# Where the high and low parts of chunk 3's split operands are issued in the opening of a fused FNet and GEGLU kernel

## The chip, the cores and the metric

The kernel runs on one core of one Trainium2 chip. The metric is the device time of one execution in microseconds (us); a shorter time is better. The engines are named as in the profile: PE is the matrix engine (TensorE), PEld its weight loads, DVE is VectorE, ACT is ScalarE, POOL is GpSimd and SP is SyncE, whose queue issues most of the transfers.

## What is computed

The input x has 2048 rows of 448 columns. Each row is normalized; the normalized rows go through a two-sided Fourier transform of which the real part is kept, and through a gated network, whose output gates the transform.

```
xn = layernorm(x)
a, b = xn @ hid_re.T, xn @ hid_im.T
s = seq_re @ a - seq_im @ b
g = silu((gelu(xn @ w_gate) * (xn @ w_up)) @ w_down)
out = x + s * g
```

w_gate and w_up are 448 by 1792, w_down is 1792 by 448, and all of it is in float32.

## The kernel before

Every float32 operand of a product is kept as two parts: a high part in a reduced format (written by ACT, line 142 in `split`) and a low part that is the remainder (written by DVE, line 143 in `split`). A product is three matmuls: high by high, high by low, and low by high.

The rows of x are four chunks of 512 (c = 0 to 3), and the inner dimension of the network is 14 blocks of 128 (f), taken in pairs. The program has an opening, a middle and an end. The opening turns each chunk (transposes on PE, line 187; copies on ACT; the low part on DVE) and computes the first pair of blocks, f = 0 and 1, for every chunk in the plain way: `gateup(f, c, ...)` makes two sums of 11 matmuls each (line 361), the gate and the up product, each into a PSUM bank, and `act` follows with a gelu of the gate on ACT (line 386), the gated product gelu times up on DVE (line 389), its high part on ACT (line 390) and its low part on DVE (line 391). `act` returns the last three as functions: m, h and l below, with 0 or 1 behind them for f. `down(0, c, ...)` multiplies the result with w_down in four steps kk = 0 to 3 of six matmuls each (line 415), each into one of two banks that take turns, and ACT evicts each bank (line 422) into `po_out`, which is then stored to `gs`. A list of functions, `between`, is called one entry behind each eviction, and so sets what ACT and DVE do between two evictions.

In the middle, from the pair f = 2 and 3 on, two chunks at a time are multiplied by Strassen's scheme (`strassen`, lines 438 and 445). Its operands are combinations of the turned chunks: `combine` makes them on DVE for chunks 0 and 1, and on POOL for chunks 2 and 3 (lines 217 to 224). `t_places` and `v_places` return functions t_split(i) and v_split(i) that split one combination i = 0 to 3 each; the parts go to tiles that the profile calls xt and t_lo (high and low of t) and t_v (both of v). The first unit of Strassen forms x1 to x4 in that order; x2 needs number 1 of t and v, x3 needs 2, x4 needs 0, and 3 comes later. Splitting number 3 of v ends with two small transfers (line 255), since its lower half is copied. The end transforms along the hidden dimension (line 928) and along the sequence (lines 1112 to 1129).

The order on each engine is the order in which the code is written. The mm banks go round in turn over four: gateup(0, 3) has two of them, gateup(1, 3) the other two, then x1 and x2 take the first two again, and x3 and x4 the second two. So x3 needs the gelu of gateup(1, 3) to have read its bank, and x4 its gated product.

The place of the change is the loop over c = 2 and 3 in `fnet_geglu`. At c = 2 it ends with v_split(1) and v_split(2). At c = 3 it computes gateup(0, 3), then down(0, 2) with m0, h0, l0 of chunk 3 and the four t_split between its steps, then gateup(1, 3) with v_split(0) and v_split(3), and then m1. Behind the loop `spill(1)` stores half of chunk 3, and the last down of the pair, down(0, 3), is spread over the first units of Strassen.

Of the kernel before, what the change touches and what calls it, by code (L numbers as in the profile page):

```python
# [45 lines left out]
def fnet_geglu(ctx: ExitStack, tc: tile.TileContext, x, ca, ct, cp, et, wgu, wd, out):  # L46
# [137 lines left out]
    def turn_mm(c, k):  # L184
        pt = tp_tile(f"pt{c}_{k}").rearrange("p (b d) -> p b d", b=4)
        for b in range(4):
            nc.tensor.transpose(pt[:, b], xr[c][:, k, b * P : (b + 1) * P], ident)
        return c, k, pt
# [7 lines left out]
    def turn_split(c, k, pt):  # L196
        sl = slice(k * P, (k + 1) * P)
        h, l = [cols_of(xs(c, lo), c, sl) for lo in range(2)]
        nc.scalar.activation(h, turned(pt, c), AF.Copy)
        for i, v in enumerate(xf[c]):  # L200
            nc.scalar.activation(v[:, :, sl], pt[:, 3 * i :] if i else pt[:, : v.shape[1]], AF.Copy)
        nc.vector.tensor_sub(l, turned(pt, c), h)
# [24 lines left out]
    def t_places(p):  # L227
        if not t_lo:
            t_lo.append(sb.tile([P, 4096], FR, name="t_lo", tag="y"))
        h = [a_x[2 * p + 1][:, o : o + 512] for o in (0, 512, 2048, 2560)]  # L230
        l = [t_lo[0][:, 2048 * p + 512 * i :][:, :512] for i in range(4)]
        t_hl[p][0] = list(zip(h, l))

        def one(i):
            side, k = SPOT[i]
            split(h[i], l[i], xfk(2 * p + side, k))

        return one

    def v_places(p):  # L240
        v = sb.tile([P, 4096], FR, name=f"t_v{p}", tag=f"v{p}")
        vt[p] = v
        hl = []
        for side, k in SPOT:
            hl.append([v[:, 2048 * side + 512 * (k + 2 * a) :][:, :512] for a in range(2)])
        t_hl[p][1] = hl

        def one(i):
            side, k = SPOT[i]
            h, l = hl[i]  # L250
            n = 64 if i == 3 else P
            split(h[:n], l[:n], xfk(2 * p + side, k + 2)[:n])
            if i == 3:
                for a in (h, l):
                    nc.sync.dma_start(a[64:].bitcast(F32), a[:64].bitcast(F32))

        return one
# [7 lines left out]
    def load_s(f, i):  # L265
        raw = a_r[i]
        nc.sync.dma_start(raw[:, :1280], wgu[f].rearrange("p b f -> p (b f)"))
        return raw
# [45 lines left out]
    def prep_s(i, raw):  # L314

        w = slot(i)
        hw = w[:, :1792]
        steps = []

        def part_(a, b):  # L320
            nc.scalar.activation(hw[:, a:b], raw[:, P + a : P + b], AF.Copy)  # L321
            lo = max(a, 384)
            nc.vector.tensor_sub(  # L323
                w[:, 1408 + lo : 1408 + b], raw[:, P + lo : P + b], hw[:, lo:b].bitcast(F32)
            )
            if a == 0:
                nc.vector.tensor_sub(
                    hw[64:, :384], raw[64:, P : P + 384], hw[64:, :384].bitcast(F32)
                )

        names = "x4 x2 x3 s1 a11 a12 a22 b11 r1 s3 s2 s4 r3 r2".split()
        parts = {}
        for n, name in enumerate(names):
            parts[name] = [w[:, n * P : (n + 1) * P]]
            if n > 2:
                parts[name].append(w[:, 1408 + n * P : 1408 + (n + 1) * P])
        return parts, [lambda: part_(0, 896), lambda: part_(896, 1792)]

    def load_d(grp, at):
        rv = at[:, : 2 * D].rearrange("p (f d) -> p f d", f=2)  # L340
        nc.sync.dma_start(
            rv, wd[grp[0] * P : (grp[0] + 2) * P, :].rearrange("(f p) d -> p f d", p=P)
        )
        return rv
# [37 lines left out]
    def act(f, c, pg):  # L382
        acts[0] += 1
        gt = tmp(2 + acts[0] % 2)
        hs = new_hs(f, c)
        nc.scalar.activation(gt, pg[0], AF.Gelu_apprx_tanh)

        return (
            lambda: nc.vector.tensor_mul(gt, gt, pg[1]),
            lambda: nc.scalar.activation(hs[:, 0], gt, AF.Copy),  # L390
            lambda: nc.vector.tensor_sub(hs[:, 1], gt, hs[:, 0]),
        )

    def gateup(f, c, w, between=()):
        pg = gu_ps(f, c)
        for g in range(2):
            gu_mm(pg[g], w, g, c, slice(0, 512))
            if g < len(between):
                between[g]()
        return act(f, c, pg)  # L400
# [28 lines left out]
    def down(gi, c, wdn, between=()):  # L429
        for kk in range(4):  # L430
            down_one(gi, c, wdn, kk)
            if kk < len(between):
                between[kk]()
# [82 lines left out]
    with tc.manual_schedule():  # L516
# [113 lines left out]
        m0, h0, l0 = act(0, 0, pgs[0])  # L630
# [17 lines left out]
        m0, h0, l0 = act(0, 1, pg)  # L648
# [11 lines left out]
        def spill(p):  # L660
            nc.sync.dma_start(xp[p], x_half(p))
# [34 lines left out]
        for c in (2, 3):  # L696
            if c == 2:
                draw = load_d(GROUPS[1], a_st[:, 2304:])
            else:
                s_raw2 = load_s(GROUPS[1][1], 1)  # L700
            m0, h0, l0 = gateup(0, c, ws[0])
            if c == 2:
                turn = lambda k: turn_split(*turn_mm(3, k))
                between = [
                    lambda: (m0(), h0(), norm(2)),
                    lambda: (l0(), norm(3), turn(0), comb.pop(0)()),
                    lambda: (turn(1), comb.pop(0)()),
                    lambda: (turn(2), comb.pop(0)()),
                ]
                between1 = [lambda: (turn(3), comb.pop(0)())]  # L710
            else:
                t_split = t_places(0)
                between = [
                    lambda: (m0(), h0(), t_split(1)),
                    lambda: (l0(), t_split(2)),
                    lambda: t_split(0),
                    lambda: t_split(3),
                ]
                between1 = [lambda: v_split(0), lambda: v_split(3)]
            down(0, c - 1, wdn, between)  # L720
            if c == 2:
                nws[0], steps = prep_s(0, s_raw)
                for f in steps:
                    f()
            m1, h1, l1 = gateup(1, c, ws[1], between1)
            m1()
            if c == 2:
                h1()
                l1()
                comb.pop(0)()  # L730
                v_split = v_places(0)
                v_split(1)
                v_split(2)
        spill(1)
        late = (h1, l1)

# [568 lines left out]
```

## Time and profile before

| what | value |
|---|---|
| median of 3 runs | 783.08 us (782.25 to 785.52) |
| the profiled execution's own time | 782.91 us |
| span of the profiled execution | 781.1 us |
| PE busy | 766.0 us, 98% of the span, 4044 instructions |
| DVE busy | 545.3 us, 70% |
| ACT busy | 363.8 us, 47% |
| POOL busy | 189.1 us, 24% |
| moved by DMA | 170.05 MB, 218 GB/s on average |

The time of an execution is 1.81 us longer than its span. A busy time counts from the start of an instruction to its modelled end; matmuls overlap, so the distance from one start to the next says more about PE's rate than a matmul's own duration. In the rows of the timeline the columns are start, duration, engine, line, operation, what is written and read, the shapes and the count; in brackets stands how long the engine was idle ahead of it and what ended that.

### The profile page before, as it was taken

How to read it: one execution, taken by the hardware profiler on the slowest of the kernel's cores; microseconds unless marked ns; L12 is line 12 of the kernel's file. 1: busy time of each engine (PE TensorE's matmuls, PEld its weight loads, DVE VectorE, ACT ScalarE, POOL GpSimd, SP SyncE). 2: the span in 40 equal slices, each digit the busy share in tenths (PEclk: the TensorE clock that was granted, in tenths of full speed). 3: DMA queues.
4: the chain of work that ended last, by engine and by line, in shares of the span. 5: the costliest groups of instructions: out<-in, count | busy, mean ns of one | idle time of the engine just before them, and what ended most of it. 6: DMA issues, size and time to landing. Idle time of an engine off the chain costs nothing.

```text
span 781.1 us, 11376 instructions
## 1 busy us (share of the span) xinstructions
PE 766.0 (98%) x4044; PEld 686.4 (88%) x4044; DVE 545.3 (70%) x937; ACT 363.8 (47%) x538; POOL 189.1 (24%) x308
## 2 busy tenths in 40 slices
PE   8998999999999999999999999999999999999997
PEld 7887888888888888888889999999999989998896
DVE  7888677545565556456452767988879696969687
ACT  3884545444434435344444585544344433434341
POOL 1119025240421511601011001223222231313130
PEclk9999999999999999999999999999999999999999
DMA  7232656995978968774989972869696959787784
GB/s 289 92 118 88 202 199 131 274 178 108 252 136 219 276 115 218 179 166 81 259 214 247 372 318 82 273 225 329 199 362 192 353 184 315 229 286 226 274 266 180
DMA packets 61371, 170.05 MB, mean 218 GB/s; under 512 B 7425, under 2 KB 40065, under 8 KB 60417
## 3 DMA queue, kind: packets, MB, share of 16 engines
q1 hardware_dynamic: 47440, 108.17, 39.2%
q0 software_dynamic: 13728, 61.02, 34.1%
q8 instruction: 32, 0.52, 0.3%
q14 instruction: 27, 0.21, 0.1%
q10 hardware_dynamic: 144, 0.11, 0.0%
HBM read 127.21 MB, written 70.91 MB: 254 GB/s over the span
## 4 chain that ended last, share of the span: by engine, by line
PE 69%; DVE 15%; DMA 10%; issue 3%; ACT 1%; SPq 0%; DVEq 0%; ACTq 0%
PE x L438 23%; PE po L415 16%; PE ab L928 9%; PE p L1112 8%; PE x L445 4%; PE p L1115 4%; DVE xt L143 4%; DVE e L143 3%; DMA w<-td 3%; PE gu L361 3%; DMA raw<-ct 2%; DMA tmp<-ct 2%; DMA raw<-wgu 1%; DMA raw_d<-ct 1%; DVE cc L1150 1%
## 5 line engine op out<-in xcount | busy, mean ns | idle before, releaser
L438 PE MATMUL x<-xt,w 128*128 128x512 f32 x480 | 149.5, 392 | 0.0
L438 PEld LDWEIGHTS x<-xt,w 128*128 128x128 f32 x480 | 90.1, 188 | 16.1 <-DVE tmp L477 0.4
L422 ACT ACTIVATE po_out<-po 128x448 f32<-128x448 f32 x112 | 60.2, 538 | 83.7 <-PE po L415 82.8
L415 PE MATMUL po<-wd0h,hs 128*128 128x448 f32 x256 | 82.0, 367 | 3.1 <-ACT po_out L422 3.1
L427 POOL DMA_DIRECT2D gs<-po_out x24 | 21.4, 893 | 219.2 <-ACT po_out L422 219.1
L928 PE MATMUL ab<-e,xt 128*128 128x448 f32 x288 | 68.8, 365 | 0.0
L415 PE MATMUL po<-wd,hs 128*128 128x448 f32 x288 | 66.0, 365 | 0.0
L438 PE MATMUL x<-t_v,w 128*128 128x512 f32 x216 | 60.7, 389 | 0.0
L415 PEld LDWEIGHTS po<-wd,hs 128*128 128x128 f32 x288 | 54.1, 188 | 6.7
L928 PEld LDWEIGHTS ab<-e,xt 128*128 128x128 f32 x288 | 54.1, 188 | 4.3
L415 PEld LDWEIGHTS po<-wd0h,hs 128*128 128x128 f32 x256 | 48.1, 188 | 8.4 <-ACT po_out L422 3.5
L1007 POOL DMA_DIRECT2D raw<-sums x45 | 24.8, 552 | 98.4 <-DVE xt L143 29.4
L438 PEld LDWEIGHTS x<-t_v,w 128*128 128x128 f32 x216 | 40.5, 188 | 8.7
L415 PE MATMUL po<-wd0l,hs 128*128 128x448 f32 x128 | 46.9, 366 | 0.0
L142 ACT ACTIVATE e<-raw 128x896 fp32r<-128x896 f32 (+1 forms) x30 | 27.7, 923 | 34.0 <-DVE raw L1014 22.9
L1112 PE MATMUL p<-t_v,wd0l 128*128 128x448 f32 x112 | 37.5, 380 | 3.6 <-DVE cc L1209 3.6
L493 ACT ACTIVATE hs<-tmp 128x512 fp32r<-128x512 f32 x24 | 15.2, 635 | 54.9 <-DVE tmp L491 54.9
L438 PE MATMUL x<-t_lo,w 128*128 128x512 f32 x96 | 37.3, 389 | 0.0
L1007 POOL DMA_DIRECT2D tmp<-sums x39 | 21.5, 552 | 63.6 <-DVE xt L143 27.7
L1112 PE MATMUL p<-w,e 128*128 128x448 f32 x112 | 36.6, 375 | 0.1
L323 DVE TENSOR_TENSOR w<-raw,w 128x512 fp32r<-128x512 f32 (+1 forms) x24 | 21.3, 889 | 19.9 <-ACT w L321 19.9
L143 DVE TENSOR_TENSOR e<-raw,e 128x896 fp32r<-128x896 f32 (+1 forms) x30 | 31.4, 1047 | 4.3 <-ACT e L142 4.0
(317 smaller groups left out, 2014.5 us busy)
## 6 DMA issues: line engine op xcount, KB each, us to landing
gs<-po_out POOLq DMA_DIRECT2D x24, 896.0 KB, 7.9
sums<-ca SPq DMA_DIRECT2D x16, 896.0 KB, 10.7
sums<-ca POOLq DMA_DIRECT2D x16, 896.0 KB, 14.5
t_v<-td SPq DMA_DIRECT2D x24, 448.0 KB, 5.5
w<-td SPq DMA_DIRECT2D x24, 448.0 KB, 7.0
raw<-ct SPq DMA_DIRECT2D x45, 192.0 KB, 4.5
raw<-wgu SPq DMA_DIRECT2D x12, 640.0 KB, 5.5
tmp<-ct SPq DMA_DIRECT2D x39, 192.0 KB, 4.7
```

The source lines that it names most:

```text
L142: nc.scalar.activation(h, src, AF.Copy)
L143: nc.vector.tensor_sub(l, src, h)
L361: nc.tensor.matmul(ps[:, cols], a, xt[:, cols], start=n == 0, stop=n == len(mm) - 1)
L415: nc.tensor.matmul(po[:, :D], hs[:, a, kk * P : (kk + 1) * P], wdn[b][:, i], start=n == 0, stop=n == 5,)
L422: nc.scalar.activation(out_[0][:, kk], po[:, :D], AF.Copy)
L427: nc.gpsimd.dma_start(gv[:, 4 * c : 4 * c + 4], out_[0], accum_op=ALU.add)
L438: nc.tensor.matmul(ps, a[i], b[j], start=first and n == 0, stop=n == 2, skip_group_check=True)
L445: nc.tensor.matmul(ps, a[0], xt, start=False, stop=True, skip_group_check=True)
L928: nc.tensor.matmul(p[:, :D], a, b, start=n == 0, stop=n == len(mm) - 1)
L1007: nc.gpsimd.dma_start(v[:, 4 * P : 6 * P], sums[j][:, KS.index(k)])
L1112: nc.tensor.matmul(ps[q][:, :D], h, v, start=u % UN == 0, stop=False, skip_group_check=True)
L1115: nc.tensor.matmul(ps[q][:, :HD], l, v[:, :HD], start=False, stop=u % UN == NS - 1, skip_group_check=True,)
```

## The change

At c = 2, v_split(2) is taken out of the end of the pass. At c = 3 it stands behind the first eviction of down(0, 2), next to m0, which had stood there with h0 and t_split(1). h0 and t_split(1) move behind the second eviction. l0 and t_split(2) stay behind the third; t_split(0) moves from there to behind the fourth, with t_split(3). No instruction is added, dropped or altered.

```
             else:
                 t_split = t_places(0)
                 between = [
-                    lambda: (m0(), h0(), t_split(1)),
+                    lambda: (m0(), v_split(2)),
+                    lambda: (h0(), t_split(1)),
                     lambda: (l0(), t_split(2)),
-                    lambda: t_split(0),
-                    lambda: t_split(3),
+                    lambda: (t_split(0), t_split(3)),
                 ]
                 between1 = [lambda: v_split(0), lambda: v_split(3)]
             down(0, c - 1, wdn, between)
...
                 comb.pop(0)()
                 v_split = v_places(0)
                 v_split(1)
-                v_split(2)
```

Since l0 was second in the list and is now third, one entry is added ahead of it and two at the end are made one. On ACT this changes the rows from the last instructions of the pass c = 2 to the four evictions of down(0, 2). po_2_0 to po_2_3 are the four steps of that down, gu_3_0 is the gate of chunk 3 for f = 0, hs<-tmp is h0, t_v<-xf is the high part of a v_split, and xt<-xf that of a t_split.

```order
-L142 ACTIVATE t_v_694<-xf_72 128x512 x2
-L386 ACTIVATE tmp<-gu_3_0_700 128x512
-L422 ACTIVATE po_out<-po_2_0_726 128x448
+L142 ACTIVATE t_v_694<-xf_72 128x512
+L386 ACTIVATE tmp<-gu_3_0_698 128x512
+L422 ACTIVATE po_out<-po_2_0_724 128x448
+L142 ACTIVATE t_v_694<-xf_72 128x512
+L422 ACTIVATE po_out<-po_2_1_735 128x448
 L390 ACTIVATE hs_79<-tmp 128x512
 L142 ACTIVATE xt_67<-xf_72 128x512
-L422 ACTIVATE po_out<-po_2_1_738 128x448
+L422 ACTIVATE po_out<-po_2_2_746 128x448
```

Ahead of the eviction of po_2_1 stood h0 and the high part of t_split(1); now the high part of v_split(2) stands there, and h0 and t_split(1) come behind it.

On DVE the same place is short. tmp<-tmp,gu_3_1 is m0, t_v<-xf,t_v is the low part of a v_split, t_lo<-xf,xt that of a t_split, and hs<-tmp,hs is l0.

```order
-L143 TENSOR_TENSOR t_v_694<-xf_72,t_v_694 128x512 x2
-L389 TENSOR_TENSOR tmp<-tmp,gu_3_1_701 128x512
+L143 TENSOR_TENSOR t_v_694<-xf_72,t_v_694 128x512
+L389 TENSOR_TENSOR tmp<-tmp,gu_3_1_699 128x512
+L143 TENSOR_TENSOR t_v_694<-xf_72,t_v_694 128x512
 L143 TENSOR_TENSOR t_lo<-xf_72,xt_67 128x512
 L391 TENSOR_TENSOR hs_79<-tmp,hs_79 128x512
```

m0 has one low part ahead of it instead of two; the other low part follows it. The rows of PE, POOL and SP stand in the same order as before.

More of the change, by code (lines that the diff above doesn't have):

```diff
@@ L713, in fnet_geglu @@
                 between = [
-                    lambda: (m0(), h0(), t_split(1)),
+                    lambda: (m0(), v_split(2)),
+                    lambda: (h0(), t_split(1)),
                     lambda: (l0(), t_split(2)),
-                    lambda: t_split(0),
-                    lambda: t_split(3),
+                    lambda: (t_split(0), t_split(3)),
                 ]
@@ L732, in fnet_geglu @@
                 v_split(1)
-                v_split(2)
         spill(1)
```

## Prediction

> **What bounds the kernel now.** I read the page first: which engine fills the span.
>
> ```profile
> PE 766.0 (98%) x4044; PEld 686.4 (88%) x4044; DVE 545.3 (70%) x937; ACT 363.8 (47%) x538; POOL 189.1 (24%) x308
> ```
>
> PE is busy for 98% of 781.1 us, so only a gap of PE, or fewer matmuls, can change the time. The change leaves the matmuls as they are. So I asked next what PE waited for (total us, times, longest):
>
> ```profile
> PE p L1112 <- DVE cc L1209: 3.6, 4, 1.0
> PE po L415 <- ACT po_out L422: 3.1, 1, 3.1
> ```
>
> Beside the start of the program there are two waits of size: four of about 1 us late in the program, and one of 3.1 us. The second is a down step that waits for an eviction on ACT. Is PE otherwise at its rate? Three stretches of the windows (us, then busy us and instructions of PE, PEld, DVE, ACT and POOL, the granted clock, the DMA share and GB/s):
>
> ```profile
> 72.20:79.00 6.80, 6.80 (x31) 5.75 (x32) 6.16 (x8) 4.05 (x8) 6.72 (x10) 1.00 0.41 154
> ...
> 200.00:300.00 100.00, 100.00 (x459) 85.86 (x459) 57.05 (x78) 43.56 (x76) 30.70 (x54) 1.00 0.84 202
> 300.00:400.00 100.00, 100.00 (x459) 85.89 (x458) 55.16 (x80) 43.42 (x76) 19.53 (x31) 1.00 0.78 185
> ```
>
> Two different stretches of 100 us hold 459 matmuls each with PE busy throughout: the middle is paced by PE alone, and what PE saves ahead of it is handed on unchanged. Now the chain that ended last, around the wait of 3.1 us:
>
> ```profile
> 66.40 3.46 DVE t_v L143 x2
> 69.86 0.61 DVE tmp L389
> ```
>
> The reader sees the path: two low parts on DVE (of v_split(1) and v_split(2)), then m0. The next pieces of the chain are ACT's, whose rows follow below: h0, the high part of t_split(1), and only then the eviction for which PE stands. These are the instructions that the change moves.
>
> **What goes.** The timeline of PE shows the size:
>
> ```profile
> 67.43 0.57 PE L415 MATMUL po<-wd0h,hs 128*128 128x448 f32 x2
> ...
> 68.45 0.37 PE L415 MATMUL po<-wd0l,hs 128*128 128x448 f32 x1
> 68.65 0.36 PE L415 MATMUL po<-wd0h,hs 128*128 128x448 f32 x1
> 72.12 0.47 PE L415 MATMUL po<-wd0h,hs 128*128 128x448 f32 x1 [3.11 <-ACT po_out L422]
> 72.43 0.36 PE L415 MATMUL po<-wd0l,hs 128*128 128x448 f32 x1
> ...
> 73.45 5.18 PE L361 MATMUL gu<-xt,wd 128*128 128x512 f32 x22
> ...
> 82.54 0.39 PE L438 MATMUL x<-xt,w 128*128 128x512 f32 x1
> ```
>
> Matmuls of this shape start 0.20 us apart (68.45 to 68.65). The first matmul of po_2_3 starts 3.47 us behind its forerunner, so 3.27 us are lost; the next one starts 0.31 us later instead of 0.20, another 0.11. Together 3.38 us. The printed 3.11 is less, because it counts from the modelled end of the last matmul; it is the lower end, and 3.47 the upper. I take 3.38.
>
> **Does the eviction really come in time?** ACT's rows:
>
> ```profile
> 66.62 0.55 ACT L422 ACTIVATE po_out<-po 128x448 f32<-128x448 f32 x1 [2.13 <-PE po L415]
> 70.49 0.63 ACT L390 ACTIVATE hs<-tmp 128x512 fp32r<-128x512 f32 x1 [3.33 <-DVE tmp L389]
> 71.03 0.61 ACT L142 ACTIVATE xt<-xf 128x512 fp32r<-128x512 f32 x1
> 71.55 0.53 ACT L422 ACTIVATE po_out<-po 128x448 f32<-128x448 f32 x1
> ...
> 91.46 0.61 ACT L142 ACTIVATE xt<-raw 128x512 fp32r<-128x512 f32 x1
> ```
>
> The eviction of po_2_0 starts at 66.62 in both versions, since PE sets it. Behind it now comes the high part of v_split(2), about 0.6 us as in the row at 71.03: 67.1 to 67.7. Its input was combined long before; its old place was ahead of the gelu of chunk 3. po_2_1's last matmul is the first of the pair at 67.43 and ends at about 67.80 (0.37 behind its start), so its eviction runs from 67.84 to 68.4. PE wants the bank at 68.85 and loads weights about 0.2 ahead of that. The wait is gone, with some 0.25 us to spare. Should the eviction be 0.5 us later (the high part behind it or ACT late by its own length), PE would lose about 0.3 us of the 3.38.
>
> **What waits newly.** h0 now stands ahead of the eviction of po_2_2 and waits for m0. On DVE:
>
> ```profile
> 66.40 3.46 DVE L143 TENSOR_TENSOR t_v<-xf,t_v 128x512 fp32r<-128x512 f32 x2
> 69.79 0.67 DVE L389 TENSOR_TENSOR tmp<-tmp,gu 128x512 f32<-128x512 f32 x1
> 71.67 1.21 DVE L143 TENSOR_TENSOR t_lo<-xf,xt 128x512 fp32r<-128x512 f32 x1 [1.22 <-ACT xt L142]
> 72.80 0.94 DVE L391 TENSOR_TENSOR hs<-tmp,hs 128x512 fp32r<-128x512 f32 x1
> 73.67 2.68 DVE L143 TENSOR_TENSOR t_lo<-xf,xt 128x512 fp32r<-128x512 f32 x3
> 76.28 1.81 DVE L143 TENSOR_TENSOR t_v<-xf,t_v 128x512 fp32r<-128x512 f32 x2
> 78.73 0.69 DVE L389 TENSOR_TENSOR tmp<-tmp,gu 128x512 f32<-128x512 f32 x1 [0.64 <-PE gu L361]
> ```
>
> One low part takes half of 3.46, that is 1.73, and ends at 68.13. m0 then runs to about 68.8, h0 to 69.35, the high part of t_split(1) to 69.9, and the eviction of po_2_2 follows at once. Nobody misses it: its bank is next written by down(0, 3), after x4. The other ACT work keeps its order and is done before its reader: the high parts of t_split(0), t_split(3), v_split(0) and v_split(3) end near 73.4, and the gelu of gateup(1, 3) behind them, 0.6 us, near 74, while x3, which takes its bank, starts at 77.8 (82.54 less six matmuls 0.228 us apart, less 3.38; the spacing is that of the row of 22, 5.18 less one of 0.39, over 21).
>
> DVE is the tight one. Its work does not shrink: only its idle 1.22 us goes. From 68.8: the low part of v_split(2) at 1.73 ends at 70.5; that of t_split(1), pulled back beside POOL's large instructions, I also put at 1.73, to 72.2; l0 0.9, to 73.1; three low parts of t at 0.87 (2.61 of start distance, 73.67 to 76.28), to 75.7; two of v at 0.9, to 77.5; m1 at 0.67, to 78.2. Before, m1 waited for PE (0.64 idle); now it is set by DVE. x4 needs its bank, and starts at 82.54 - 3.38 = 79.16, its weights 0.2 ahead. So 0.75 us are left, and a cost of nothing for PE. Where this cover goes, each us of DVE beyond 0.75 is a us of PE. x2 needs the low part that ends at 72.2, and starts at 76.4; x4 needs one that ends near 76.6. Behind m1 DVE's queue is about 0.8 us late on PE's time, and PE needs the next of its sums, that of x3, only where the second product into that bank starts, 17 matmuls behind x4's first (about 82.9), against 81.3 by the same sum (x2's sum, l1, one low part and x3's sum behind m1).
>
> **POOL** sets how long DVE's instructions take:
>
> ```profile
> 69.40 1.59 POOL L223 TENSOR_TENSOR raw<-raw,xf 128x512 f32<-128x512 f32 x1
> 71.07 1.27 POOL L224 TENSOR_TENSOR xf<-xf,raw 128x512 f32<-128x512 f32 x1
> 72.29 0.91 POOL L303 TENSOR_TENSOR raw<-raw 128x128 f32<-128x128 f32 x1
> ...
> 79.45 0.46 POOL L312 TENSOR_TENSOR raw<-raw 128x128 f32<-128x128 f32 x1
> ```
>
> Beside the 128x512 instructions of POOL a low part takes 1.73, beside the 128x128 ones 0.87 to 0.9; m0, which reads PSUM, took 0.67 even while POOL was in its row at 69.40. After the change only the low parts of v_split(2) and t_split(1) meet large ones. POOL ends near 80.2, since its own instructions meet DVE's a little longer. What waits for it is a copy of weights on ACT for the next Strassen unit, whose first matmul stands 33 behind x4's, near 86: hidden.
>
> [...]
>
> **SP** keeps its order. The store of half of chunk 3 stands behind two small transfers of v_split(3), which follow DVE:
>
> ```profile
> 78.64 0.59 SPq L661 DMA_DIRECT2D xp<-xt  x1
> ...
> xp<-xt SPq DMA_DIRECT2D x1, 1024.0 KB, 4.4
> ```
>
> So the store is issued about 0.5 us earlier, not 3.38. It lands 4.4 us behind its issue, by 82.6; the high part that overwrites that half runs at 91.46 - 3.4 = 88.1. Hidden, with over 5 us.
>
> **Sum.** 782.91 - 3.38 = 779.53, say **779.5 us** for the profiled execution (its span 781.1 and the 1.81 around it). The median of the runs, 783.08, is 0.17 higher, so that the ratio to it is about 0.995.
>
> **The clock.** Behind the gap the granted clock is 1.00 (72.20:79.00), and starts are at once 0.2 apart again (six matmuls from 72.12 to 73.45 take 1.33, of which 0.11 is in the sum). So the gap has no tail. [...]
>
> **The rivals.**
> - **DVE late for x4.** If the three low parts of t also take 1.73 and not 0.87, m1 ends 2.6 us later and x4 waits 2.6 - 0.75 = 1.85: 781.4. For it: DVE has no idle left from 66.4 to 78.2. Against it: those rows run beside 128x128 instructions of POOL in both versions. With smaller delays the time lies between 779.5 and 781.4.
> - **The other side: DVE's queue takes more than PE gets back.** If all five low parts behind l0 take 1.73, m1 comes 4.2 us later and x4 waits 3.45, already more than 3.38. DVE's sums for x3 and x4 then come late as well for the second products into those banks, up to about 1 us by two more such low parts: 784.0. It decides from a DVE delay of 3.38 + 0.75 = 4.1 us on. POOL's short rows speak against it.
> - **The change doesn't do what it says.** ACT reaches the eviction of po_2_1 late all the same, or another wait stands behind this one on the same matmul: 782.9. ACT's idle 3.33 ahead of h0, which ended with m0, speaks against it.
> - **A tail of the gap.** Were the 3.47 us behind the gap at half rate, 1.7 more would go: 777.8. The clock row speaks against it.
> - **The end shifts.** The four waits near 1 us in the end hang on DVE and on transfers that land in a new phase: 1 us either way, 778.5 or 780.5.
>
> **How the numbers follow.** Forecast, 779.2 to 779.9: 0.77. DVE late: 0.09. The other side: 0.03. No effect: 0.04. Tail: 0.01. End shifted: 0.06, half each way. The range from 778.4 to 781.6 leaves out the slow side, no effect and the tail, and some scatter: the three runs before lie 3.3 us apart, and the median of the next ones carries part of that. 0.5%, about what a measurement of this kernel can tell from no change, is 3.9 us, or 779.2: the forecast lies just inside it. Of its 0.77 I give 0.21 to a measured time beyond that, with 0.01 and 0.03 from the tail and the end: faster 0.25. Slower by 0.5%, over 787, is in none of the cases; 0.03 for what I have missed. Within: 0.72.
>
> **What would show it.** In the profile after, PE's wait for po_out L422 is gone; the evictions of po_2_0 and po_2_1 start near 66.6 and 67.8, and the 22 matmuls of gateup(1, 3) start near 70.1, not 73.45. m0 starts near 68.2, and m1 ends near 78.2. x4 starts at 79.2 without a wait. I am wrong if PE waits for L389 at x4 or for the splits at x2 or x3, if the eviction of po_2_1 starts later than 68.3, or if the 3.4 us are there at 100 us and not at the end.

## The result and the profile after

The changed kernel takes 778.16 us (median of 19 runs, 775.14 to 784.24), the kernel before 784.34 us (median of 19 runs, 780.26 to 787.1). The ratio is 0.9929, with a 95% interval from 0.9914 to 0.9944: 5.6 us less (4.4 to 6.7). The forecast was 3.4 us less, with a chance of 0.72 that the change stays within 0.5% and of 0.25 that it is faster than that. The whole interval lies beyond 0.5%, so the less likely of the two came. The direction and the place were right; the gain is larger than the sum.

The profile after is one execution of 778.02 us with a span of 776.3. First its waits of PE (engine, line, what it waited for: total us, times, longest):

```profile
PE p L1111 <- DVE cc L1208: 2.8, 5, 1.0
PE warm L538 <- DVE hs L528: 1.5, 1, 1.5
PE gu L361 <- DVE xt L202: 0.4, 1, 0.4
```

The wait of 3.1 us for `po_out` is gone and no other has come in its place. The rows of PE from the end of po_2_2 on (the second matmul of the pair at 68.17 is the first of po_2_3), in the timeline of the changed kernel:

```profile
68.17 0.57 PE L415 MATMUL po<-wd0h,hs 128*128 128x448 f32 x2
68.58 0.36 PE L415 MATMUL po<-wd0l,hs 128*128 128x448 f32 x1
...
69.59 5.18 PE L361 MATMUL gu<-xt,wd 128*128 128x512 f32 x22
74.61 1.75 PE L438 MATMUL x<-xt,w 128*128 128x512 f32 x7
...
78.69 0.39 PE L438 MATMUL x<-xt,w 128*128 128x512 f32 x1
```

The 22 matmuls of gateup(1, 3) start at 69.59 instead of 73.45, and x4 at 78.69 instead of 82.54. Of these 3.86 us, 0.48 lie ahead of the place (gateup(0, 3) starts at 59.74 here and at 60.22 in the first profile, a difference of the program's first 15 us); 3.38 are the gap. ACT's rows in the same execution:

```profile
66.14 0.55 ACT L422 ACTIVATE po_out<-po 128x448 f32<-128x448 f32 x1 [2.65 <-PE po L415]
66.58 0.62 ACT L142 ACTIVATE t_v<-xf 128x512 fp32r<-128x512 f32 x1
67.42 0.55 ACT L422 ACTIVATE po_out<-po 128x448 f32<-128x448 f32 x1 [0.22 <-PE po L415]
68.32 0.63 ACT L390 ACTIVATE hs<-tmp 128x512 fp32r<-128x512 f32 x1 [0.36 <-DVE tmp L389]
```

The high part of v_split(2) ends ahead of the second eviction, which now waits for PE (0.22) and not the other way round. DVE's rows:

```profile
67.62 0.67 DVE L389 TENSOR_TENSOR tmp<-tmp,gu 128x512 f32<-128x512 f32 x1
68.22 1.41 DVE L143 TENSOR_TENSOR t_v<-xf,t_v 128x512 fp32r<-128x512 f32 x1
69.56 1.78 DVE L143 TENSOR_TENSOR t_lo<-xf,xt 128x512 fp32r<-128x512 f32 x1
71.26 1.78 DVE L391 TENSOR_TENSOR hs<-tmp,hs 128x512 fp32r<-128x512 f32 x1
72.97 2.68 DVE L143 TENSOR_TENSOR t_lo<-xf,xt 128x512 fp32r<-128x512 f32 x3
75.58 1.81 DVE L143 TENSOR_TENSOR t_v<-xf,t_v 128x512 fp32r<-128x512 f32 x2
77.32 0.67 DVE L389 TENSOR_TENSOR tmp<-tmp,gu 128x512 f32<-128x512 f32 x1
```

m1 ends at 77.99, which is 78.47 with the 0.48 added back, and x4 takes its bank 0.7 us later without a wait. So the gap explains 3.4 of the 5.6 us. The experiments search for the rest.

### The profile page after: what moved, and what is told of

It reads as the page before. It is cut to its first block, busy times and chain, and to the rows that moved or that the text cites. A ratio compares the mean times of both kernels' runs of the same rounds, so it can differ in the third digit from the quotient of the medians.

```text
span 776.3 us, 11377 instructions
## 1 busy us (share of the span) xinstructions
PE 765.2 (99%) x4044; PEld 686.3 (88%) x4044; DVE 546.8 (70%) x937; ACT 363.6 (47%) x538; POOL 189.0 (24%) x308
## 4 chain that ended last, share of the span: by engine, by line
PE 83%; DVE 8%; DMA 5%; issue 2%; ACT 1%; SPq 0%; DVEq 0%; ACTq 0%
PE x L438 23%; PE po L415 17%; PE p L1111 16%; PE ab L927 9%; PE p L1114 8%; PE x L445 4%; PE gu L361 3%; DVE e L143 2%; DVE xt L143 1%; DMA raw<-wgu 1%; DMA raw_d<-ct 1%; DMA w<-td 1%; DMA raw<-ct 1%; DMA raw<-cp 1%; PE py L1126 1%
```

## The experiments

Three theories were on record ahead of them. **Stall**: the change is worth its gap, 3.4 us, and the rest is scatter. **Tail**: in some executions PE's clock falls behind the gap, and that goes too. **End**: being earlier by 3.4 us shortens the waits of the last stage. The time from the first matmul of line 415 to the first of line 438 (two starts of the timeline) separates the opening's last part from the rest; the time from the first matmul of line 1112 to the last matmul shows the last stage. The diffs are against the kernel before where nothing else is said.

**The changed kernel again** (e1_after), with no edit.

> The changed kernel once more, beside the kernel before on the same chip. Stall theory: the change gives back the 3.38 us of PE's gap and no more, a ratio near 0.9957; what lies beyond it in the first comparison (0.9929) is scatter of the start and of the end. Tail theory: the gap of 3.47 us costs more than its length in some executions, because PE runs slower for a while behind it; the ratio stays near 0.993 and the profile after shows no wait of 1 us in other places than before. End theory: being earlier by 3.4 us moves the waits of the last stage, and the ratio stays near 0.993 with fewer or shorter waits there (5.0 us of late starts over 0.3 us before, counted from 480 us on).

It ran at 0.9949 of the kernel before (0.9930 to 0.9967; 4.0 us less, 2.6 to 5.5). That interval holds the stall theory's 3.4 and, together with the first comparison, leaves 4.4 to 5.5 us as what both allow. Its last stage took 289.8 us, against 290.2 in the first profile of before. This alone decided nothing.

**h0 and t_split(1) moved alone** (e2_h0_alone):

```
-                    lambda: (m0(), h0(), t_split(1)),
+                    lambda: m0(),
+                    lambda: (h0(), t_split(1)),
                     lambda: (l0(), t_split(2)),
-                    lambda: t_split(0),
-                    lambda: t_split(3),
+                    lambda: (t_split(0), t_split(3)),
```

> The second half of the change alone: v_split(2) stays at the end of the pass c = 2, so that m0 still has two low parts ahead of it on DVE; h0 and t_split(1) stand behind the second eviction. The eviction of po_2_1 then has nothing of DVE ahead of it on ACT. If the order on ACT is the cause, PE's wait goes entirely (gain 3.4 us, as with the whole change), the eviction of po_2_1 starts near 67.8 and m0 near 69.8, and m1 ends near 78.8, only 0.2 us ahead of x4's weights. If m0's place on DVE is the cause, 1.7 us of the wait or more remain.

0.9943 (0.9925 to 0.9960), 4.5 us less (3.1 to 5.9): within the noise the same as the whole change. The timeline of ACT in this run shows why:

```profile
66.43 0.55 ACT L422 ACTIVATE po_out<-po 128x448 f32<-128x448 f32 x1 [2.12 <-PE po L415]
67.71 0.55 ACT L422 ACTIVATE po_out<-po 128x448 f32<-128x448 f32 x1 [0.73 <-PE po L415]
70.33 0.63 ACT L390 ACTIVATE hs<-tmp 128x512 fp32r<-128x512 f32 x1 [2.07 <-DVE tmp L389]
```

h0 still stands idle for m0 until 70.33, as in the kernel before, but the two evictions are ahead of it. The order on ACT is the cause; the move of v_split(2) isn't needed for it. All that the move buys is cover on DVE: m1 ends 0.70 us ahead of x4 with it and 0.38 us without (78.60 against 78.98 in this run).

**v_split(2) moved alone** (e3_v2_alone):

```
-                    lambda: (m0(), h0(), t_split(1)),
+                    lambda: (m0(), v_split(2), h0(), t_split(1)),
...
                 v_split(1)
-                v_split(2)
```

> The first half alone: v_split(2) stands behind m0, but h0 and t_split(1) stay ahead of the eviction of po_2_1. m0 near 68.2, h0 near 68.8, the high part of t_split(1) to 69.9, the eviction of po_2_1 from 69.9 to 70.4: PE's gap falls from 3.47 to about 1.8 us, a gain of 1.7 us. If the order on ACT didn't matter, the gain would be 3.4.

0.9958 (0.9943 to 0.9973), 3.3 us less (2.1 to 4.5). PE's rows of this run:

```profile
68.58 0.36 PE L415 MATMUL po<-wd0h,hs 128*128 128x448 f32 x1
70.35 0.47 PE L415 MATMUL po<-wd0h,hs 128*128 128x448 f32 x1 [1.41 <-ACT po_out L422]
```

The gap is 1.77 us, as expected, and po to x1 is shorter than in the first profile by 1.68 us. But 2.1 to 4.5 us were measured, and 1.68 is below the interval.

**The same delay without a gap** (e4_busy17). 17 matmuls fill the place of the gap in the changed kernel; the first real matmul overwrites their result:

```
+        if (gi, c, kk) == (0, 2, 3):
+            hs = hs_of[0, c]
+            for _ in range(17):
+                nc.tensor.matmul(
+                    po[:, :D], hs[:, 0, kk * P : (kk + 1) * P], wdn[0][:, 0], start=True, stop=True
+                )
```

> The changed kernel with 17 more matmuls of 128x448 at the place of the old gap (their result is overwritten by the first real matmul of po_2_3): 17 x 0.2025 = 3.44 us in which PE is busy where it stood idle before. All that follows comes as late as in the kernel before, but PE has no gap. Stall theory: as slow as the kernel before, within 0.3 us of the sum. Tail theory: 3.4 us above the changed kernel, but about 2 us below the kernel before. End theory: as slow as the kernel before, since the end lies where it lay, with the waits of before in the last stage.

0.9970 (0.9954 to 0.9986), 2.4 us less than the kernel before (1.1 to 3.6). From x1 to the last stage every matmul starts as late as in the first profile of before, within 0.01 us, and yet the time isn't that of before. The stall theory and the end theory both wanted the time of before. What the kernel before pays beyond its delay hangs on PE being idle. The last stage of this execution was even the longer one, 292.4 us against 290.2. The size is less sure than the sign: the tail theory put this kernel 3.4 us above the changed one, and its median of 781.51 (12 runs, 778.87 to 784.66) is only 1.9 above the 779.65 of e1_after (6 runs, 778.7 to 782.6).

**The kernel before, profiled again** (e5_before, e6_before, e7_before, e10_before, e11_before, e12_before), with no edit.

> The kernel before once more under the profiler; the first four runs left it 2 us slower than the gap of PE explains (the busy delay in e4 gave back only part of what the change took). Tail theory: in this execution or in one of the next two the granted clock falls behind the gap at 72 us, and the 33 matmuls behind it take longer than the 7.5 us of the first profile. End theory: the gap is 3.47 us with no tail, and the late starts of the last stage (4.7 us in the first profile, 3.1 and about 5.5 in two of the changed kernel) are larger than in the changed kernel, around 6 us. Scatter theory: the gap has no tail, the late starts lie between 3 and 6 us as in the changed kernel, and the time differs from the changed kernel's profiles by 3.4 us on average.

> A second look at the same kernel, for the scatter of the gap and of the late starts in the last stage from one execution to the next; the same three expectations as for e5_before.

> A third look at the same kernel; the same three expectations as for e5_before.

> A fourth look at the kernel before, on the same chip as the two others, for the share of executions with the fall of the clock: 42.3 us from the first po to x1 without, 43.8 with it. [...]

> A further look at the kernel before, for the share of executions in which the clock falls behind the gap (so far four of five profiles). [...]

> One more look at the kernel before. [...]

All six differ from the first profile, and in the same way. The windows of e6_before, in the stretches around the gap (columns as in the prediction):

```profile
68.50:72.00 3.50, 0.39 (x3) 0.14 (x2) 2.29 (x3) 1.78 (x4) 3.34 (x3) 1.00 0.00 0
72.00:79.00 7.00, 7.00 (x25) 5.82 (x26) 6.72 (x7) 3.97 (x8) 6.80 (x11) 0.76 0.40 150
79.00:92.00 13.00, 13.00 (x61) 10.95 (x60) 7.90 (x12) 4.76 (x8) 0.00 (x0) 1.00 0.77 256
```

PE is busy throughout the seven us behind the gap, but the granted clock is 0.76 and 25 matmuls fit where the first profile has about 31. 0.76 over 7 us is 3.4 us at half the clock (7 x 0.24 / 0.5). The matmuls show it directly, in PE's timeline of e6_before:

```profile
68.18 0.37 PE L415 MATMUL po<-wd0l,hs 128*128 128x448 f32 x1
68.39 0.36 PE L415 MATMUL po<-wd0h,hs 128*128 128x448 f32 x1
71.86 0.57 PE L415 MATMUL po<-wd0h,hs 128*128 128x448 f32 x1 [3.11 <-ACT po_out L422]
72.22 0.57 PE L415 MATMUL po<-wd0l,hs 128*128 128x448 f32 x1
72.60 0.95 PE L415 MATMUL po<-wd0h,hs 128*128 128x448 f32 x2
73.34 0.57 PE L415 MATMUL po<-wd0l,hs 128*128 128x448 f32 x1
```

The gap is the same 3.47 us. Behind it the matmuls start 0.38 us apart (72.22 to 72.60) and take 0.57, where ahead of it they start 0.21 apart (68.18 to 68.39) and take 0.36. All executions with the gap of 3.47, and the others beside them:

| execution | first po to x1, us | granted clock, 72 to 79 us | last stage, us |
|---|---|---|---|
| before, first profile | 42.26 | 1.00 | 290.2 |
| e5_before | 43.81 | 0.76 | 288.5 |
| e6_before | 43.83 | 0.76 | 290.2 |
| e7_before | 43.80 | 0.77 | 291.2 |
| e10_before | 43.82 | 0.76 | 289.7 |
| e11_before | 43.75 | 0.79 | 290.8 |
| e12_before | 43.79 | 0.77 | 292.4 |
| after | 38.86 | 1.00 | 289.2 |
| e1_after | 38.87 | 0.999 (whole execution) | 289.8 |
| e2_h0_alone | 38.85 | 0.999 (whole execution) | 290.3 |
| e3_v2_alone | 40.58 | 1.00 (68 to 76 us) | 292.4 |
| e4_busy17 | 42.32 | 1.00 | 292.4 |

Six of seven executions of the kernel before have the tail, and it costs 43.80 - 42.26 = 1.54 us. None of the kernels without the gap, or with 1.77 us of it, has one in its one profile (for e1 and e2 this is read from 38.87 and 38.85 us, which match the 38.86 of after). That the gap can have a tail came as expected; why one execution of seven has none is not shown by these runs. The last section says what the traces show of the clock.

From x1 to the first matmul of the last stage (407 us), all 1888 matmuls stand at the same distance from x1 in every profile of this case as in the first, within 0.04 us. So the profiles differ only ahead of x1 and in the last stage. That scatters between 288.5 and 292.4 us in the seven profiles of before, which average 290.4, and between 289.2 and 292.4 in the other five of the table; the three without any delay (after, e1, e2) average 289.8. Nothing here supports the end theory, and e4 speaks against it: 0.6 us between the averages is less than the scatter. A shift of that size can't be ruled out either.

**The gap of before, filled** (e8_fill15). 15 matmuls run in the gap into a bank that nobody reads; the wait for the eviction stays as it is:

```
+        if (gi, c, kk) == (0, 2, 3):
+            fill = tp_tile("fill")
+            for _ in range(15):
+                nc.tensor.matmul(
+                    fill[:, :D], hs_of[0, c][:, 0, :P], wdn[0][:, 0], start=True, stop=True
+                )
```

> The kernel before, with 15 matmuls of 128x448 put into the gap ahead of po_2_3, into a bank that nobody reads (15 x 0.2025 = 3.04 us, within the 3.27 us lost there). The first matmul of po_2_3 still waits for the same eviction and starts at the same time, so PE's order and every wait are those of before; only PE is not idle. Three of four profiles of the kernel before showed the granted clock at 0.5 for 3.41 us behind the gap, and 43.8 us from the first po to x1 in place of 42.26. Tail theory: no fall of the clock here, 42.3 us from po to x1, and 1.0 to 1.55 us less than the kernel before (a ratio of 0.998 to 0.9987). Stall theory: the same time as before (the end's scatter of 2 us may hide either in part).

0.9974 (0.9950 to 0.9999), 2.0 us less (0.1 to 3.9). PE's timeline:

```profile
68.55 3.20 PE L410 MATMUL fill<-wd0h,hs 128*128 128x448 f32 x15
71.84 0.47 PE L421 MATMUL po<-wd0h,hs 128*128 128x448 f32 x1
72.14 0.36 PE L421 MATMUL po<-wd0l,hs 128*128 128x448 f32 x1
72.35 0.57 PE L421 MATMUL po<-wd0h,hs 128*128 128x448 f32 x2
```

po_2_3 starts at 71.84, as late as in e6_before (71.86), but its matmuls then start 0.21 apart, the clock stays at 1.00, and po to x1 is 42.28 us, the first profile's value. The useless work on PE saves the tail.

**The tail in the timed runs.** Each timed run has one number for the clock, the mean granted over the execution, rounded to 0.001. A tail of 3.4 us at half the clock lowers it by 0.0022 (3.4 x 0.5 / 784). On the chip of e1 to e4 the median is 0.997 over the 17 runs of before and 0.999 or 1.000 in each of the four kernels beside them; on the chip of e8_fill15 it is 0.996 over 23 runs of before against 0.998 over 12. The averages, without one odd run of 0.95 in either set, lie 0.0017 and 0.0018 apart, about four fifths of a tail: an estimate, but the timed runs have the tail too, in about the share of the profiles.

**The gap doubled** (e9_gap7). A low part is computed two more times on DVE ahead of m0, with the same values:

```
                 v_split(1)
                 v_split(2)
+                for _ in range(2):
+                    h_, l_ = t_hl[0][1][2]
+                    nc.vector.tensor_sub(l_, xfk(1, 2), h_)
```

> The kernel before, with the low part of v_split(2) computed two more times on DVE ahead of m0 (the same values are written again): the gap grows by 2 x 1.73 = 3.46 to about 6.9 us. [...] Time against the kernel before: 3.5 to 5 us more (tail theory, by the share of its executions that have the tail already), 3.5 (stall theory).

1.0047 (1.0026 to 1.0069), 3.7 us more than the kernel before (2.0 to 5.4), and 47.00 us from po to x1. The windows:

```profile
68.00:75.00 7.00, 0.78 (x4) 0.38 (x2) 5.72 (x5) 1.40 (x3) 6.84 (x9) 0.74 0.00 0
75.00:82.00 7.00, 6.76 (x24) 5.73 (x25) 5.93 (x7) 4.36 (x9) 2.75 (x5) 0.77 0.39 147
```

Now the clock is already down inside the gap (0.74) and stays down behind it: the two rows together are 6.9 us at half the clock, twice the length of before. The part that PE feels is of the same kind, 47.00 - 42.26 - 3.35 = 1.4 us, where 3.35 is the growth of the gap (6.82 less 3.47).

**Both terms together.** The gap is 3.40 us between first profile and after (42.26 - 38.86), the tail 1.54 in six executions of seven, 1.32 on average: 4.7 us. The measured intervals against this sum and against the gap alone:

| kernel | measured, us against before | gap alone | gap and tail |
|---|---|---|---|
| changed, first comparison | -5.6 (-6.7 to -4.4) | -3.4 | -4.7 |
| e1_after | -4.0 (-5.5 to -2.6) | -3.4 | -4.7 |
| e2_h0_alone | -4.5 (-5.9 to -3.1) | -3.4 | -4.7 |
| e3_v2_alone | -3.3 (-4.5 to -2.1) | -1.7 | -3.0 |
| e4_busy17 | -2.4 (-3.6 to -1.1) | +0.1 | -1.3 |
| e8_fill15 | -2.0 (-3.9 to -0.1) | 0.0 | -1.3 |
| e9_gap7 | +3.7 (+2.0 to +5.4) | +3.4 | +3.4 |

The sum with the tail lies in all seven intervals; the gap alone misses four of them. The seven aren't independent: e1 to e4 share 17 runs of the kernel before, and e8 and e9 share 23. (For e9 the two agree here, because the gap alone counts no tail on either side, and with it the tail of 1.4 meets one of 1.3.)

## Why the prediction was right, and where it fell short

- **What bounds the kernel.** PE alone, in the middle: right. From x1 to the last stage the first two profiles run at one distance within 0.02 us, and what was saved at 72 us is still saved there.
- **The gap.** 3.38 us in the sum; 3.40 from po to x1 in the profiles. Right to a few hundredths.
- **The order on ACT as its cause.** Right, and e2 shows that the move of h0 and t_split(1) does it alone. The eviction of po_2_1 started at 67.42, or 67.9 with the 0.48 added back, where 67.84 was forecast.
- **m0 earlier by one low part.** Right in its times (67.62, or 68.1 for 68.2) but worth nothing on top of the other move, since no eviction that PE needs soon is behind h0 any more. With h0 left where it was (e3) it is worth 1.68 us of the gap.
- **DVE's cover ahead of x4.** Forecast 78.2 for the end of m1, measured 78.47 on the same scale; l0 took 1.78 us where 0.9 was put, and the low part of v_split(2) 1.41 where 1.73 was. The prediction let only two low parts meet POOL's 128x512 instructions; l0 (71.26 to 73.04) met the last of them too, which ran from 70.87 to 72.50 on POOL. The cover held with about 0.5 us (0.7 less the 0.2 for the weights).
- **The tail: the step that failed.** The prediction read "So the gap has no tail" off the one profile it had, gave the tail 0.01, and set its price at 1.7 us. No run shows the 3.47 us at half rate that this price counts with; that was the author's estimate. What the runs showed in its place is 3.4 us at half the clock (0.76 over 7 us in e6_before), which cost 1.54 us. So the price was near, but the chance was wrong: six of seven executions of the kernel before have the tail, and the profile at hand was the seventh. Whether this gap has the tail changes from one execution to the next, so one execution can't settle it.
- **The end.** It scatters by up to 4 us from execution to execution, so a shift of 1 us either way, as the prediction priced it, can be neither seen nor ruled out.

The measured 778.16 us lies a quarter of a us under the low end of the range, 778.4. With the tail at its average of 1.32 us the same sum, from the median of before that the comparison itself shows, gives 784.34 - 4.72 = 779.6, within the scatter of the runs; from the first profile, which had no tail, nothing but the gap could come out. For the same reason it is luck that 777.8, the prediction's time with a tail, lies near the measured one: it takes a tail off 782.91, an execution that had none. Of the 5.6 us, 0.9 more than the sum is inside the measured interval (4.4 to 6.7) and not explained further.

## What to carry to other kernels

Where an engine that runs in the order written, as ACT did here (the eviction of po_2_1 came at 71.55, behind h0 at 70.49, with its bank done at 67.80), both evicts banks and waits for another, put the eviction ahead of the instruction that waits: only the order on ACT mattered here, and half the change did the whole work (4.5 us less in e2, 4.0 in e1). Price a gap of PE as its length plus the slow stretch that executions of the same kernel show behind it (here a gap of 3.47 us, and 1.54 us more in six executions of seven), and profile several executions before calling that stretch absent. The shorter gap of e3, which left PE idle for 1.4 us, didn't lower the clock (1.00 from 68 to 76 us). If a gap like the one here can't be removed, matmuls into an unread bank in its place may save the tail, as in e8 (42.28 us from po to x1, against 43.80).

## What the runs showed of the hardware

At the gap of 3.47 us between two starts the granted clock was at half for 3.4 us in each of two executions. In e6_before it was 1.00 from 68.50 to 72.00 and 0.76 from 72.00 to 79.00 (7 x 0.24 / 0.5); in e12_before it was 0.96 from 68.50 to 72.00, 0.61 from 72.00 to 76.00 and 1.00 from 76.00 to 79.00, so that 0.3 us of the 3.4 lie ahead of 72.00 and 3.1 behind it. At the gap of 6.82 us in e9_gap7 it was at half for 6.9 us, of which 3.6 lie ahead of 75.00 (0.74 from 68.00 on), inside the gap, which ended at 75.23. A gap of 1.77 us left it at 1.00 in the one profile that has it, and the gap of 3.47 us left it at 1.00 in the first profile of before, from 68.65 to 72.12 and from 72.12 to 79.00.

Behind the last matmul of the program the clock fell as well. In the profile after, that matmul ends at 771.12 by its modelled end; the clock is 1.00 from there to 773.20 and 0.50 from 773.30 to 776.20. In the first profile of before it ends at 776.02, and the clock is 1.00 from there to 780.80 and 0.50 from 780.90 on. So PE had been idle for some 2.1 us ahead of the fall in the one and 4.8 us in the other: in these traces the length of the idle time alone doesn't tell when the clock falls. What else sets it isn't shown, and neither is why six of seven executions with the same gap have the tail.
